# Block-sparse attention with a low-rank mixer: other queues for the first loads, first row copies cut by key chunk, pair 5 loaded earlier

## The chip, the cores and the metric

The kernel runs on one core of a Trainium2 chip. The metric is the device time of one execution in microseconds. Before the change, five runs gave a median of 284.89 us (283.51 to 286.13).

The engines are named as in the profile: PE is TensorE (matmuls; PEld is its weight load), DVE is VectorE, ACT is ScalarE, POOL is GpSimd and SP is SyncE. SP, ACT and POOL each have a queue from which DMAs are issued.

## The reference

Batch 4, 8 heads, 768 positions, head dimension 64. Attention is limited to blocks of 32: neighbours, the first and last row and column of blocks, and three sampled blocks in each row. Its output goes through a low-rank mix over positions and an MLP over 512 channels.

```python
mask = np.abs(blk_i - blk_j) <= 1
mask = mask | (blk_i == 0) | (blk_j == 0) | (blk_i == n_blocks - 1) | (blk_j == n_blocks - 1)
for qb in range(n_blocks):
    for kb in sampled_blocks[qb]:
        mask[qb * block:(qb + 1) * block, kb * block:(kb + 1) * block] = True
scores = np.where(mask, scale * np.matmul(q, k.transpose(0, 1, 3, 2)), -1e9)
attn = softmax(scores)                      # rows of 768
x = np.matmul(attn, v)                      # heads side by side: 4 x 768 x 512
u = x + (x.transpose(0, 2, 1) @ U @ V).transpose(0, 2, 1)       # rank 32
out = u + np.maximum(u @ w_ch1, 0.0) @ w_ch2                    # 512 -> 2048 -> 512
```

(`softmax` stands for the maximum, exponential, sum and division that the reference writes out.)

## The kernel before

**Tiling.** The heads are taken in pairs, 16 pairs in all, four for each batch entry. A sequence is laid out as 128 partitions by `T` = 6. For each head and each chunk `g` of 128 keys, PE multiplies the turned keys with the turned queries into PSUM (128 keys by 768 queries), ACT takes the exponential into a slot of `est`, and PE multiplies this by the values, with a column of ones that gives the sum (`value_product`, L400). DVE divides (`divide`, L472 and L477: one reciprocal and two products for each head).

**Two ways to mask.** For batch entry 0 (pairs 0 to 3) the mask is added by the matmul itself. The queries' tile `qres` has, beside the 64 data rows of a head, 24 rows with a one-hot code of the query's block, and the keys' tile `kres` has 24 rows with a bias of 0 or -240 for each key and query block. The bias is made at the start. `neq`, `a01` and `bias` (L289, L293, L296) come from the sampled blocks and from the constants in `small`. Two matmuls `mask_half` (L271) spread them over the 768 keys, and `mask_row` (L279) copies the result into the mask rows of `kres[0]`, for each head and each half of the keys. For pairs 4 to 15 the scores are unmasked, two chunks at once (`half_quad`, L741), and DVE multiplies the exponentials by a 0/1 mask (L756) that `mask_part` (L656, L662) makes during pairs 0 to 3.

**The start.** The first head of pair 0 is loaded by itself. `first_load` issues its DMA, `first_cast` converts it to 16 bits into `sts`, `first_turn` (L224) turns 3 chunks of 128 positions on PE, and `first_row` (L282) copies the turned rows into `qres[0]` or `kres[0]`. Eight matmuls on constants (`keep_warm`, L264) run on PE before that. The second head of pair 0 follows by `last_turn` (L337) and its copy (step `z`, L344). `second_set` copies the mask rows to `kres[1]` and `kmask` by DMA. The identity for turning, `id16`, lies in the same tile and the same DMA as the mask constants (`small`, 128 rows of 356 bytes).

**Order.** Inside `manual_schedule` each engine runs its instructions in the order in which the program issues them. After the start this order is the string `PLAN`, one word for each step, and a digit is the PSUM bank (of 8) that the step writes. Capitals are PE steps and small letters are the steps that empty them: `S` is a score block (2 banks) and `B` two blocks at once (3 banks), each with its exponential `e`; `A` is a value product of six matmuls, with `v` for the division; `R` is the turn of a later pair's queries or keys, with `t` for the row copies; `K`/`k` is a part of the 0/1 mask; `Z`/`z` is the turn of pair 0's second head; `M`/`m`, `X`, `Y`/`y`, `D`/`d` and `E`/`g` belong to the mix; `Q`, `H` are scores of pairs 4 to 15, with `e` and the mask product `p`; `V` is their value product; `U`, `P`, `C` are the first MLP matrix (L587) with relu `a` on ACT or `b` on DVE; `W`/`f` is the second (L611, L619).

**Loads.** `loads(i)` issues pair i+2's queries, keys and values on SP and casts them on POOL. From pair 5 on, `front(i+1)` ahead of it issues two DMA transposes of that pair's queries and keys. `begin(i)`, called when the first score of pair i is taken up, decides which loads are issued there. Pair 5's `loads(3)` is issued at the start of pair 3, and `front(5)` and `hold` (which lets POOL issue the `w2t` loads behind a copy that waits for pair 5's transposed keys) at the start of pair 4. The DMA transposes of the turned activations `uT` (L544) are on SP, too.

Of the kernel before, what the change touches and what calls it, by code (L numbers as in the profile page):

```python
# [12 lines left out]
FP32 = mybir.dt.float32  # L13
FP16 = mybir.dt.float16
# [5 lines left out]
P = 128  # L20
# [3 lines left out]
def kernel(  # L24
# [14 lines left out]
    nc = tc.nc  # L39
# [28 lines left out]
    small_np = np.zeros((P, NB + 1 + P // 2), np.float32)  # L68
    small_np[:NB, :NB] = (ms_np - 1.0) * -MASK_BIAS
    small_np[:NB, NB] = ii  # L70
    small_np[:, NB + 1 :] = np.eye(P, dtype=np.float16).view(np.float32)

    small_dr = nc.inline_tensor(small_np, name="small_const")
    ohT_dr = nc.inline_tensor(ohT_np, name="one_hot_const")
# [36 lines left out]
    small = consts.tile([P, NB + 1 + P // 2], FP32)  # L111
    ms = small[0:NB, 0:NB]
    iota = small[0:NB, NB : NB + 1]
    id16 = small[:, NB + 1 :].bitcast(FP16)
# [54 lines left out]
    def first_load(h, n, queue):  # L169

        src, nm = ((q, "qld"), (k, "kld"))[n]
        if h == 0:
            lds[nm] = ldpool.tile([P, 2, T, D], FP32, tag="ld" + nm, name=nm)
            sts[0, nm] = stpool.tile([P, T, 2, D], FP16, tag="st" + nm, name="st" + nm)
        if h == 1:
            nc.gpsimd.memset(lds[nm][0:1, h, 0, 0:1], 0.0)
        queue.dma_start(
            out=lds[nm][:, h], in_=src[0, h].rearrange("(p t) d -> p t d", t=T)
        )

# [4 lines left out]
    bias = consts.tile([P, 2, D], FP16)  # L185
    for vt in vts:
        nc.gpsimd.memset(vt[:, :, :, D : D + 1], 1.0)
# [3 lines left out]
    def second_set():  # L191
        for h in range(2):
            one_hot(1, h)
            nc.sync.dma_start(out=kres[1][mrows[h], h, :], in_=kres[0][mrows[h], h, :])
        nc.sync.dma_start(out=kmask[mrows[0], :], in_=kres[0][mrows[0], 0, :])
# [12 lines left out]
    def first_cast(h, n, copy):  # L208
        nm = ("qld", "kld")[n]
        copy(out=sts[0, nm][:, :, h], in_=lds[nm][:, h])  # L210
# [3 lines left out]
    def first_turn(n, c):  # L214

        if n == 1:
            pt = psm([P, HS], FP32)
        elif c == 0:
            pt = pw[:, 1, 0:HS]
        else:  # L220
            pt = psc2()[:, 0, 0:HS]
        first_out[n, c] = pt
        for j in range(3):
            nc.tensor.matmul(  # L224
                pt[0:D, j * P : (j + 1) * P],
                sts[0, ("qld", "kld")[n]][:, 3 * c + j, 0],
                id16,
                start=(j == 0), stop=(j == 2), skip_group_check=True,
            )

    with tc.manual_schedule(
# [13 lines left out]
        first_load(0, 0, nc.sync)  # L245
        nc.scalar.dma_start(out=small, in_=small_dr.ap())
        first_load(0, 1, nc.scalar)
        for h in (1, 0):
            nc.vector.memset(qres[0][(slice(D, P), slice(0, D))[h], h, :], 0.0)
            one_hot(0, h)  # L250
        nc.vector.memset(bias, 0.0)
# [26 lines left out]
        def mask_row(h, c, copy):  # L278
            copy(out=kres[0][mrows[h], h, c * HS : (c + 1) * HS], in_=pks[c][mrows[h]])  # L279

        def first_row(n, c, copy):
            copy(  # L282
                out=(qres, kres)[n][0][drows[0], 0, c * HS : (c + 1) * HS],
                in_=first_out[n, c][0:D],
            )

        neq = consts.tile([P, NB, 3], FP32)
# [14 lines left out]
        for n in range(2):  # L302
            first_cast(0, n, nc.vector.tensor_copy)
        for c in range(2):
            first_turn(0, c)
            first_row(0, c, nc.scalar.copy)
        mask_half(0)
        mask_row(0, 0, nc.vector.tensor_copy)
        first_turn(1, 0)
        first_row(1, 0, nc.scalar.copy)  # L310
        first_turn(1, 1)
        mask_half(1)
        keep_warm(2, 256)
        first_row(1, 1, nc.vector.tensor_copy)
        mask_row(0, 1, nc.vector.tensor_copy)
        mask_row(1, 0, nc.vector.tensor_copy)
        mask_row(1, 1, nc.vector.tensor_copy)
# [3 lines left out]
        nc.vector.memset(Ut, 0.0)  # L321
        load_v(0)
        load_qk(1)
        second_set()
        load_v(1)
        load_mix()


# [105 lines left out]
    S0 S3 e e S5 B0 e Z7 e S3 z Z6 e z B0 A7 A e R6 S3 t A R5 e A B0 t A K6 e A S3 k v A5 A e K6  # L434
    k B0 A A e K7 A K6 k S3 k A K7 e v B0 k S3 e M6 e A5 A m R7 A t B0 K6 R3 e k A A t S6 A e v
    S0 D2 S3 e d A7 A e A S0 K6 A e S3 k K2 A e S5 k A e v S3 R2 e S5 t S0 e M7 e S3 m D2 e B5 d
    A0 D1 e A A d A S3 D2 A e d K1 S5 k R7 e S3 t A S1 e v A5 A e A S3 S6 e K2 A e A k A S3 v B0
    e K7 M6 e k S3 m X5 K7 e A6 Y k A B0 y X7 Y e S3 y E5 A e A g A R7 S0 t A e v S4 S2 e A7 A e
    R1 E6 A t A g A A Q v e e M6 X7 m Y P6 y p H U7 e p H b C e p H b U7 e p H b U6 e p E1 a g p
    V7 Q v e e V6 U7 v p U0 a P1 b C p P6 a C E7 Q a g U6 e e U7 b P6 b p U0 C a U7 p a Q b X6 Y  # L440
    e e P7 y C P6 b C p U0 b a p V7 Q v e e V6 W7 v p U0 W a p Q U6 e e W b U6 p W b p Q f W6 e
    e W p U2 U0 a p a V7 Q v W e e p V7 U2 v W a p Q f W7 e e W p U6 W a p Q U6 e e W b U6 p f a
    p V0 U1 v a V7 U6 v Q a M6 e e W7 m W p D6 U0 d U1 p a D2 D3 a U6 d d D0 U5 a d D6 U1 a d W
    a W Q f D6 W7 e e d W p D0 D6 W d d p W Q f W6 e e W p W W p Q f e e V7 U6 v p a V0 U2 v p
    U7 a U6 a Q b U7 e e U6 b U7 b p U2 a U6 p a U7 a Q b U6 e e U7 b U6 b p U2 a p a V7 Q v e e
    V6 U7 v p U0 b U1 a W6 p a Q W e e W p W U7 f p Q a U6 e e W7 b W p U1 p a V6 Q v W e e p V6
    U2 v W a p Q f W6 e e W p U7 W b p Q U7 e e W b U7 p f U2 a p a V0 v V7 W6 v Q M7 e e W m U7
    p D0 U1 a d U2 p a D7 D3 a U0 d d U1 a D5 D0 a U2 d d U7 a W a W Q f D7 W6 e e d W p D1 D7 W
    d d p W Q f W7 e e W p W W p Q f e e V6 U7 v p a V0 U2 v p U7 a U6 a Q b U7 e e U6 b U7 b p
    U2 a U6 p a U7 a Q a U6 e e U7 b U6 b p U2 a p a V7 Q v e e V6 U7 v p U0 a U1 a U6 p a U7 a  # L450
    Q a W6 e e W p W U7 p Q a W e e W7 f p U0 b p V6 Q v W e e W p W U6 f p Q a U7 e e W6 b W p
    p V7 Q v W e e W p U7 f U0 a p a V1 v V3 U7 v U6 a M0 b U7 m U2 a D6 U0 a d D5 U1 a d D7 W4
    a d D6 D0 D1 d D2 d D3 d W d d U6 W a W W6 f W W W W7 f W W W U6 f U0 a U1 a U7 a U6 a U4 a
    U7 b U1 a U4 a W6 a W U7 U0 a U1 a U2 a U7 a U3 a U0 a U7 a U1 a U5 a U7 a W a U7 W a W4 f W
    U7 W b W U7 f U6 a U0 b U7 a W6 b U0 W b U7 U0 b W a U0 U7 b U1 b W a L4 f W2 l W W W W4 f W
    W W L7 f l
# [327 lines left out]
    def begin(i):  # L784
# [3 lines left out]
        if i == HP:  # L788
# [4 lines left out]
        for m in {0: (0,), 1: (1, 2), 3: (3,), 4: (4,)}.get(i, ()):  # L793
            loads(m)
        if i == HP:
            hold(kpl[1])
# [56 lines left out]
    with tc.manual_schedule(  # L853
# [7 lines left out]
        for word in PLAN.split():  # L861
# [39 lines left out]
```

## Time and profile before

| What | us |
|---|---|
| median of 5 runs | 284.89 (283.51 to 286.13) |
| profiled execution, time | 283.38 |
| its span | 281.5 |
| exponentials of two blocks (L724), x9, each | 1.45 to 1.47 |
| row copies of a later pair (L686), two for queries or keys | 1.11 to 1.14 |
| first MLP matrix (L587), x512, busy | 94.3 |
| second MLP matrix (L611), x368, busy | 87.1 |

The span runs from the first to the last instruction of the profiled execution, and its time has some 1.9 us more around it. Rows of the profile name the engine, the line, the operation, the tile written and the tiles read, and their shape; in square brackets stands how long the engine was idle before and which instruction released it. "ACTq" or "SPq" is the issue of a DMA from that queue. Matmuls overlap, so a row of six has a shorter time than the sum of its parts.

### The profile page before, as it was taken

What the parts mean: (1) busy time and instruction counts of PE and PEld (TensorE: products, weight loads), DVE (VectorE), ACT (ScalarE), POOL (GpSimd) and SP (SyncE); (2) the same over time, 40 slices, a digit from 0 to 9 for tenths busy, and PEclk for the clock granted to TensorE, in tenths of its full rate; (3) what the DMA queues carried; (4) which work ended last, traced back from release to release, by engine and by line L of the source; (5) the groups of instructions that cost most, each with busy time, mean ns of one, the idle gap of its engine ahead of it and who ended that gap; (6) DMA issues with size and microseconds to landing.
All of it is one profiled execution on the core that took longest, in us unless ns stands there. A gap on an engine that the chain in (4) does not pass through costs nothing.

```text
span 281.5 us, 6704 instructions
## 1 busy us (share of the span) xinstructions
PE 273.5 (97%) x2768; PEld 159.8 (57%) x2768; DVE 194.3 (69%) x347; ACT 177.9 (63%) x206; POOL 74.0 (26%) x164
## 2 busy tenths in 40 slices
PE   7899999999999999999999999999999999999993
PEld 3577775656465654656455654656547645555552
DVE  5699988988777898788677888776677871003411
ACT  3999998888668655686867555797776303451100
POOL 5378115905634050074352050060000000000000
PEclk9999999999999999999999999999999999999999
DMA  5799997999581653646351843740001062002021
GB/s 167 238 276 303 188 256 183 191 243 225 202 231 40 188 165 98 182 111 198 85 178 40 251 104 95 210 106 7 37 37 40 17 134 77 0 0 77 0 93 57
DMA packets 49119, 37.53 MB, mean 133 GB/s; under 512 B 30465, under 2 KB 45601, under 8 KB 49089
## 3 DMA queue, kind: packets, MB, share of 16 engines
q1 hardware_dynamic: 45968, 32.61, 41.5%
q0 software_dynamic: 2688, 4.19, 8.8%
q8 instruction: 21, 0.34, 0.5%
q10 hardware_dynamic: 432, 0.31, 0.3%
q14 instruction: 10, 0.07, 0.1%
HBM read 27.67 MB, written 6.29 MB: 121 GB/s over the span
## 4 chain that ended last, share of the span: by engine, by line
PE 92%; DVE 4%; DMA 2%; issue 1%; ACT 1%; SPq 0%; DVEq 0%; ACTq 0%
PE ps L587 30%; PE ps L611 29%; PE ps L400 12%; PE ps L741 10%; PE ps L697 3%; PE ps L716 2%; PE ps L529 2%; DMA qld<-in_q_dram 1%; PE ps L656 1%; DMA out_dram<-of 1%; DVE qres L686 1%; PE ps L636 1%; PE ps L670 1%; DVE kres L279 1%; ACT est L724 1%
## 5 line engine op out<-in xcount | busy, mean ns | idle before, releaser
L750 ACT ACTIVATE est<-ps 128x1536 f16<-128x1536 f32 x72 | 100.3, 1449 | 38.7 <-PE ps L741 38.7
L587 PE MATMUL ps<-uT,w1t 128*128 128x384 f16 x512 | 94.3, 326 | 0.0
L611 PE MATMUL ps<-w2t,tT 128*128 128x512 f16 x368 | 87.1, 379 | 0.0
L756 DVE TENSOR_TENSOR est<-est,mask 128x1536 f16<-128x1536 f16 x72 | 69.7, 972 | 15.0 <-ACT est L750 14.9
L599 ACT ACTIVATE tT<-ps 128x384 f16<-128x384 f32 x90 | 43.0, 494 | 43.5 <-PE ps L587 42.3
L587 PEld LDWEIGHTS <-w1t 128*128 128x128 f16 x512 | 47.6, 98 | 36.3 <-issue 5.8
L611 PEld LDWEIGHTS <-tT 128*128 128x128 f16 x368 | 34.5, 98 | 39.6 <-issue 3.8
L400 PEld LDWEIGHTS <-est 128*128 128x128 f16 x1152 | 40.8, 97 | 7.0 <-issue 1.9
L400 PE MATMUL ps<-vt,est 128*128 128x65 f16 x1152 | 43.4, 193 | 0.0
L140 POOL CAST stqld<-qld 128x192 f16<-128x192 f32 x40 | 15.4, 426 | 85.6 <-DMA qld<-in_q_dram 59.9
L619 DVE TENSOR_TENSOR of<-xf,ps 128x512 f32<-128x512 f32 x23 | 15.7, 684 | 27.7 <-PE ps L611 25.7
L601 DVE TENSOR_SCALAR tT<-ps 128x384 f16<-128x384 f32 x38 | 21.1, 556 | 18.6 <-PE ps L587 18.0
L741 PE MATMUL ps<-qpl,kpl 64*128 64x512 f16 (+1 forms) x288 | 31.3, 325 | 0.0
L706 ACT ACTIVATE est<-ps 128x768 f16<-128x768 f32 x30 | 22.5, 813 | 0.6 <-PE ps L697 0.6
L741 PEld LDWEIGHTS <-kpl 64*128 64x128 f16 x288 | 11.8, 94 | 15.9 <-issue 10.4
L140 POOL CAST stkld<-kld 128x192 f16<-128x192 f32 x40 | 19.4, 525 | 1.4 <-PE ps L587 1.2
L477 DVE TENSOR_TENSOR xh<-ps,rcp 128x384 f16<-128x384 f32 x32 | 17.8, 558 | 1.1
L477 DVE TENSOR_TENSOR xf<-ps,rcp 128x384 f32<-128x384 f32 x32 | 17.5, 548 | 0.0
L541 DVE TENSOR_TENSOR xh<-xh,ps 128x384 f16<-128x384 f16 x28 | 15.4, 550 | 1.7 <-PE ps L529 1.6
L542 DVE TENSOR_TENSOR xf<-xf,ps 128x384 f32<-128x384 f32 x28 | 15.4, 549 | 0.0
L140 POOL CAST vt<-vld 128x192 f16<-128x192 f32 x40 | 15.1, 417 | 0.4 <-DMA vld<-in_v_dram 0.4
L697 PE MATMUL ps<-qres,kres 128*128 128x384 f16 x60 | 14.0, 324 | 0.8 <-DVE kres L279 0.5
(83 smaller groups left out, 149.3 us busy)
## 6 DMA issues: line engine op xcount, KB each, us to landing
vld<-in_v_dram SPq DMA_DIRECT2D x16, 384.0 KB, 4.6
out_dram<-of SPq DMA_DIRECT2D x23, 256.0 KB, 2.1
qld<-in_q_dram SPq DMA_DIRECT2D x15, 384.0 KB, 5.1
kld<-in_k_dram SPq DMA_DIRECT2D x15, 384.0 KB, 4.9
w1t<-in_moe_w_ch_dram POOLq DMA_DIRECT2D x4, 512.0 KB, 9.0
w2t<-in_moe_w_ch_dram POOLq DMA_DIRECT2D x4, 512.0 KB, 7.7
qld<-in_q_dram SPq DMA_DIRECT2D x2, 192.0 KB
uT<-xh SPq DMA_TRANSPOSE x14, 2.8
```

Source lines behind the costliest of these rows:

```text
L140: last = nc.gpsimd.tensor_copy(out=dst[:, h, ts], in_=ld[:, h, ts])
L400: nc.tensor.matmul(pav[:, sc, :], est[:, n, sc * P : (sc + 1) * P], vts[b % 2][:, 2 * hp + h, g, 0 : D + 1], start=(g == 0 and sc == 0), s ...
L477: nc.vector.tensor_tensor(out=dst, in0=pav[:, :, 0:D], in1=rcp[:, :, None].broadcast_to([P, T, D]), op=ALU.mult,)
L587: nc.tensor.matmul(pt, w1t[:, cc, jj * P : (jj + 1) * P], bts[b].uT[cc][:, c * HS : (c + 1) * HS], start=(cc == 0), stop=(cc == NCC - 1), ...
L599: nc.scalar.activation(out=dst, in_=pt, func=AF.Relu)
L601: nc.vector.tensor_scalar_max(out=dst, in0=pt, scalar1=0.0)
L611: nc.tensor.matmul(po, tts[b, c, jj][:, s * P : (s + 1) * P], w2t[:, jj, :], start=(jj == 0), stop=(jj == NJJ - 1),)
L697: nc.tensor.matmul(ps[:, c], kT[:, h, g * P : (g + 1) * P], qT[:, h, c * HS : (c + 1) * HS], start=True, stop=True,)
L706: lambda: nc.scalar.activation(out=dst, in_=ps, func=AF.Exp, scale=0.125),
L741: nc.tensor.matmul(units[h][:, u * S + lo : u * S + hi], kT[drows[h], g * P : (g + 1) * P], qT[drows[h], lo:hi], start=True, stop=True, sk ...
L750: nc.scalar.activation(out=both[h], in_=units[h].rearrange("p (g n) -> p g n", g=2), func=AF.Exp, scale=0.125,)
L756: lambda: nc.vector.tensor_mul(out=both[h], in0=both[h], in1=mask[:, 2 * j : 2 * j + 2, :]),
```

## The change

1. The identity leaves `small` and becomes a constant and a tile of its own (`eye_const`, `id16`, 32 KB). `small` is now 24 rows of 25 numbers, and POOL issues its DMA, ahead of its memsets.
2. ACT's queue issues the first head's queries and then `id16`. SP's queue issues the sampled blocks, the first half of the first head's keys, the two one-hot codes and the second half of the keys.
3. `first_turn` uses PE's transpose into 16-bit PSUM in place of a matmul with the identity into 32-bit PSUM.
4. The first cast of the queries goes to ACT. The keys are cast in two halves on DVE. On PE the first `mask_half` stands ahead of the turns, and the two small `keep_warm` matmuls are gone.
5. `mask_row` and `first_row` can copy a part of the columns. The first 128 keys are copied ahead of the other 256 (on ACT and on DVE).
6. The second half of the keys (`second_keys`: its turn, its rows, the mask rows of head 1, the memset of `Ut`), `second_set`, `load_v(1)`, `load_mix` and `loads(0)` are issued behind the first two scores. Both one-hot codes of the second set go ahead of the other copies.
7. `loads(3)` (pair 5) is issued at the start of pair 2, so on SP ahead of the `uT` transposes. `front(5)` and `hold` are issued at the start of pair 3.
8. `PLAN` is written anew: the same steps in the same number (but 87 relus on ACT and 41 on DVE in place of 90 and 38), in another order and with other banks. Its beginning is shown below; each of its lines differs.

```diff
-    small = consts.tile([P, NB + 1 + P // 2], FP32)
+    small = consts.tile([P, NB + 1], FP32)
     ms = small[0:NB, 0:NB]
-    id16 = small[:, NB + 1 :].bitcast(FP16)
+    id16 = consts.tile([P, P], FP16)
...
-    def first_load(h, n, queue):
+    def first_load(h, n, queue, ts=slice(0, T)):
...
         queue.dma_start(
-            out=lds[nm][:, h], in_=src[0, h].rearrange("(p t) d -> p t d", t=T)
-        )
+            out=lds[nm][:, h, ts],
+            in_=src[0, h].rearrange("(p t) d -> p t d", t=T)[:, ts],
+        )
+    halves = (slice(0, T // 2), slice(T // 2, T))
...
+    nc.gpsimd.dma_start(out=small[0:NB], in_=small_dr.ap())
...
     def second_set():
         for h in range(2):
-            one_hot(1, h)
             nc.sync.dma_start(out=kres[1][mrows[h], h, :], in_=kres[0][mrows[h], h, :])
...
-            nc.tensor.matmul(
-                pt[0:D, j * P : (j + 1) * P],
-                sts[0, ("qld", "kld")[n]][:, 3 * c + j, 0],
-                id16,
-                start=(j == 0), stop=(j == 2), skip_group_check=True,
+            nc.tensor.transpose(
+                out=pt[0:D, j * P : (j + 1) * P],
+                in_=sts[0, ("qld", "kld")[n]][:, 3 * c + j, 0],
+                identity=id16,
             )
...
-        first_load(0, 0, nc.sync)
-        nc.scalar.dma_start(out=small, in_=small_dr.ap())
-        first_load(0, 1, nc.scalar)
+        first_load(0, 0, nc.scalar)
+        first_load(0, 1, nc.sync, halves[0])
+        nc.scalar.dma_start(out=id16, in_=eye_dr.ap())
         for h in (1, 0):
             nc.vector.memset(qres[0][(slice(D, P), slice(0, D))[h], h, :], 0.0)
             one_hot(0, h)
+        first_load(0, 1, nc.sync, halves[1])
...
+        first_cast(0, 0, nc.scalar.copy)
...
         keep_warm(8)
-        for n in range(2):
-            first_cast(0, n, nc.vector.tensor_copy)
+        first_cast(0, 1, nc.vector.tensor_copy, halves[0])
+        mask_half(0)
         for c in range(2):
             first_turn(0, c)
-            first_row(0, c, nc.scalar.copy)
-        mask_half(0)
-        mask_row(0, 0, nc.vector.tensor_copy)
         first_turn(1, 0)
-        first_row(1, 0, nc.scalar.copy)
-        first_turn(1, 1)
         mask_half(1)
-        keep_warm(2, 256)
-        first_row(1, 1, nc.vector.tensor_copy)
+        mask_row(0, 0, nc.vector.tensor_copy, 0, P)
+        first_row(0, 0, nc.scalar.copy)
+        first_row(0, 1, nc.vector.tensor_copy)
+        first_row(1, 0, nc.scalar.copy, 0, P)
+        first_row(1, 0, nc.vector.tensor_copy, P)
+        mask_row(0, 0, nc.vector.tensor_copy, P)
+        first_cast(0, 1, nc.vector.tensor_copy, halves[1])
         mask_row(0, 1, nc.vector.tensor_copy)
-        mask_row(1, 0, nc.vector.tensor_copy)
-        mask_row(1, 1, nc.vector.tensor_copy)
...
-        nc.vector.memset(Ut, 0.0)
         load_v(0)
         load_qk(1)
-        second_set()
-        load_v(1)
-        load_mix()
+        for h in range(2):
+            one_hot(1, h)
+    def second_keys():
+        first_turn(1, 1)
+        first_row(1, 1, nc.vector.tensor_copy)
+        for c in range(2):
+            mask_row(1, c, nc.vector.tensor_copy)
+        nc.vector.memset(Ut, 0.0)
...
-    S0 S3 e e S5 B0 e Z7 e S3 z Z6 e z B0 A7 A e R6 S3 t A R5 e A B0 t A K6 e A S3 k v A5 A e K6
+    S0 S3 e e Z7 S0 z Z2 e B3 z S6 e B0 e e A5 A A A A A R6 v S3 t e B0 R7 e S4 t K3 A6 e A k B0
...
-        if i == HP:
+        if i == HP - 1:
             front(HP + 1)
...
-        for m in {0: (0,), 1: (1, 2), 3: (3,), 4: (4,)}.get(i, ()):
+        for m in {1: (1, 2), 2: (3,), 4: (4,)}.get(i, ()):
             loads(m)
-        if i == HP:
+        if i == HP - 1:
             hold(kpl[1])
...
-        for word in PLAN.split():
+        for x, word in enumerate(PLAN.split()):
+            if x == 2:
+                second_keys()
+                second_set()
+                load_v(1)
+                load_mix()
+                loads(0)
```

## The prediction

> **What bounds the kernel now.** I read the engines' totals and slices first, then the busy time by stage, then the first microseconds instruction by instruction.
>
> ```profile
> PE 273.5 (97%) x2768; PEld 159.8 (57%) x2768; DVE 194.3 (69%) x347; ACT 177.9 (63%) x206; POOL 74.0 (26%) x164
> ACT  3999998888668655686867555797776303451100
> ```
>
> Over the whole run TensorE is the bound, but the slices show ScalarE full from the second to the sixth. The stages, one row each (span of us, length, busy us and instructions of PE, PEld, DVE, ACT, POOL, then granted clock, DMA share, GB/s):
>
> ```profile
> 7.40:16.60 9.20, 7.89 (x106) 5.60 (x105) 6.63 (x14) 8.54 (x9) 4.83 (x6) 1.00 0.76 238
> 16.60:43.20 26.60, 26.25 (x393) 19.78 (x390) 24.08 (x55) 25.62 (x30) 11.39 (x16) 1.00 1.02 251
> 76.00:220.00 144.00, 144.00 (x1550) 81.87 (x1552) 111.00 (x183) 100.82 (x109) 35.73 (x90) 1.00 0.42 119
> 220.00:277.00 57.00, 57.00 (x372) 31.95 (x367) 19.04 (x36) 14.21 (x29) 0.00 (x0) 1.00 0.17 50
> ```
>
> From 7.4 to 43.2 us (the 48 score blocks of pairs 0 to 3) ScalarE's exponentials pace the work: it is idle for 0.66 us up to 16.6 and 0.98 us of the next 26.6. From 76 us on TensorE never pauses. So what the change does to the start counts only as far as it moves ScalarE's whole row of exponentials, and the diff leaves TensorE's later work the same in amount. The start:
>
> ```profile
> 0.79 3.47 PE L264 MATMUL ps<-const-bfloat16-1.0 128*128 128x512 bf16 x8 [0.79 <-PEq L885]
> 1.25 0.38 SPq L177 DMA_DIRECT2D qld<-in_q_dram  x1
> 3.35 0.36 SPq L177 DMA_DIRECT2D qld<-in_q_dram  x1
> 4.75 0.36 DVE L210 CAST stqld<-qld 128x384 f16<-128x384 f32 x1 [1.23 <-DMA qld<-in_q_dram]
> 5.17 0.52 PE L224 MATMUL ps<-small,stqld 128*64 128x128 f16 x6 [0.92 <-DVE stqld L210]
> 5.56 0.85 ACT L282 CAST qres<-ps 64x384 f16<-64x384 f32 x2 [2.40 <-PE ps L224]
> 6.84 0.99 PE L697 MATMUL ps<-qres,kres 128*128 128x384 f16 x5
> 7.38 2.21 ACT L706 ACTIVATE est<-ps 128x768 f16<-128x768 f32 x3 [0.59 <-PE ps L697]
> 10.42 0.56 DVE L344 COPY kres<-ps 64x768 f16<-64x768 f16 x1 [0.17 <-PE ps L337]
> 16.62 1.45 ACT L724 ACTIVATE est<-ps 128x1536 f16<-128x1536 f32 x1 [0.20 <-PE ps L716]
> ```
>
> The queries, second in SP's queue, land just before 4.75, are turned from 5.17, and the first score runs at 6.84, its exponential at 7.38. Pair 1's first exponential starts at 16.62. That is the mark by which I judge the start.
>
> **The change, step by step (us from the span's start).**
>
> *Operands.* The queries are issued on ScalarE at 0.74 instead of 1.25. From issue to landing the trace has 2.0 (the small constants, 44.5 KB) and 3.8 (the keys, 192 KB); I take 3.0, as half of the key traffic has been put off: 3.7. ScalarE has its table load and dummy behind it at 3.15. It casts the queries in 0.48 (its row of 384 columns): done at 4.2. The first half of the keys, issued on SP at 1.18, lands at 4.2 by the same 3.0, and VectorE's half cast (half of 0.36) ends at 4.4. At 3.8 instead of 3.0 the queries would be 0.7 late. At 2.0 nothing is gained, because the 8 warm-up matmuls hold TensorE until 4.26.
>
> *Mask constants on GpSimd's queue.* Now issued at 0.75. mask_half(0) is the first instruction behind the warm-up, so everything queues behind it on TensorE. Bounds from issue to landing: 2.0 (the same constants from ScalarE's queue) and 6.4 (the fastest of four 512 KB weight loads from GpSimd's queue). 25 columns of 24 rows are nearest the first; I take 2.7: 3.45, plus 0.64 for the three VectorE steps (2.89 to 3.53 in the trace) gives 4.1, in time. Landing at 6.4 would give 7.8 and put everything 3.5 later. The issue also takes GpSimd about 0.67 (its first weight-load issue), so its marker memsets of the second heads' buffers end that much later. SP's load of the second queries, which waits for one, goes out near 4.0 instead of 3.35, and the second keys, v and pair 1 behind it slip by as much. Their casts stay ahead of use: second queries land 2.2 to 3.0 later, 6.2 to 7.0, plus a cast of 0.5, against use at 7.44 below.
>
> *The skill on this queue.* The row first: four software-queue loads took 6.4 to 12.4 us for 512 KB, and no small one exists. The Trainium skill, "DMA: Bandwidth & Descriptors", section "Anatomy of one DMA — SWDGE (gpsimd) path", fits about 2.0 us plus bytes over 436 GB/s; by it the constants land at 2.8 and the sum is unchanged. Against the change stands "SBUF — State Buffer", section "SBUF: two separate sides": while VectorE runs an operation in a two-port mode, GpSimd cannot write such descriptors. If VectorE's memsets (0.89 to 2.96) counted as such, landing would be some 2.96 + 2.0 = 5.0, bias 5.6, and the start 1.4 later, an estimate from that page that would eat the lead. No row of before shows which holds.
>
> *First score.* From 4.26: mask_half 0.2, six query turns 0.36, three key turns 0.2, the second mask_half 0.2. ScalarE copies the first query half 0.39 behind its first turn (5.17 to 5.56): 4.85, for 0.43, then 128 key columns, between 0.20 (its one-column dummy) and 0.48, say 0.28: done 5.56. VectorE copies 128 mask columns (0.28, its 128-column cast at L502), then the second query half from 5.03. The new PSUM type is 16-bit: 768 such columns took 0.56, and 384 of 32-bit 0.55, so 384 of 16-bit lie between 0.28 and 0.55; I take 0.36: 5.39. First score 5.60, exponential 5.60 + 0.54 = 6.14. Lead over 7.38: 1.24. The two removed keep-warm matmuls lay in a wait and give nothing.
>
> *Where the lead goes.* VectorE's queue from there: rest of key rows 5.56 to 5.88, rest of mask rows 6.30, half cast 6.5, mask_row(0,1) 7.05, first_row(1,1) 7.40, the two mask rows of head 1 8.5, Ut 8.87, and the two z copies 9.43 and 9.99 (0.55 to 0.56 each, as L279 and L344). Z7 stands before the third score on TensorE and uses the bank that first_row(1,1) empties: 7.44, third score 7.8, exponential 8.34, though ScalarE is free at 7.62 (2 x 0.74): 0.72 idle. Z2 needs the bank that mask_row(1,1) empties: 8.54, the double score 8.9, its exponential 0.86 later (11.04 to 11.90 in the trace) at 9.76, with ScalarE free at 9.06: 0.70 idle. Then 1.45 and 0.74, so head 1's first exponential starts at 11.95; in before at 11.90. The lead is spent.
>
> *Up to pair 1.* Value products wait for the double exponential (11.21). The new order runs all six before pair 1's query turn, and VectorE does the division (0.2 + 0.56 + 0.55 = 1.16 as seen) from 12.45, then four row copies at 0.56: 15.85. Pair 1's first exponential 0.86 later, 16.7, against 16.62: +0.1. VectorE has then done a division more and a mask copy and a half less, so it stands 0.3 ahead.
>
> *Pair 5.* Its three 384 KB loads go from SP at 35.8 to behind pair 4's, before the two uT transposes (29.75 on, held 3.9 by their data). 1.15 MB at 251 GB/s is 4.6 us of DMA time put where the share is already 1.02 and w1 is loading. The cover is large: first use of w1 is at 45.3, of w2 at 68.2; pair 5's own rows are first read near 52.8. Without that cover the 4.6 would show. The uT transposes wait for VectorE anyway. GpSimd's casts of pair 5 go from 41 to near 28, where it is less than half busy (11.39 of 26.60), and the w2 loads behind its hold copies start earlier too: 0.
>
> *Rest.* Pair 4's key turn and copy (42.0 to 43.2 in before) are no longer next to the first Q, which still waits for the last value product: 0 to -0.35, I take -0.1. Three relus move from ScalarE (0.49) to VectorE (0.56), neither full there: 0. Sum: +0.1 - 0.1 = 0.0.
>
> **Own time and median.** The profiled execution took 283.38 (span 281.5 plus 1.9 around it), below the median of 284.89. With a sum of 0.0, and small slack on VectorE, 284.8 in medians.
>
> **The rivals.**
> A, likeliest: no change, 284.8. For it: VectorE's chain at 7 to 10 us and at 13 to 16. Its own range 283.7 to 286.0, by the 16-bit copies (three on the chain, -0.2 to +0.5), the landing (up to +0.7) and ScalarE's gaps (0.98 less at most).
> B, faster: ScalarE keeps the lead. If second-half copies are near 0.28 and the gaps at 7.6 and 9.1 close, -1.24, the seam -0.1, and a third of the later 0.98 idle: 284.89 - 1.7 = 283.2. For it: ScalarE has no slack in before, and any lead kept there is carried on. Against: VectorE's sum of ten operations, counted above.
> C, slower: the rewritten order starves ScalarE between 16.6 and 43.2. A reused bank that VectorE has not emptied costs 0.7, as at 7.6 and 9.1; the new order reuses banks 1 and 2 after divisions in pair 2. Three such holes: +2.1, 287.0; it decides from two. For it: VectorE busy 24.08 of 26.60. Against: I followed pairs 1 and 2 and found pair 2's first double score near 29.9 in both.
> D: the mask constants land late. Each microsecond beyond 3.6 delays the first score, and all that VectorE does behind it, by one, and the lead is spent already: from 5.0 the loss passes 1.4, and at 7.15 (0.75 + 6.4) it is 3.5, 288.3. For it: the constants stand first on TensorE now. Against: the transfer is tiny.
>
> **How the numbers follow.** A 0.48, B 0.24, C 0.20, D 0.08. About 0.5% (1.4 us) is what a measurement can tell. Faster beyond it: B but for 0.02, 0.22. Slower: C and D, 0.28. Same: 0.50. Range: A whole, down to B's 283.2 less a little, up to C's 287.0: 282.9 to 287.0.
>
> **What would show it.** First exponential near 6.1, ScalarE idle some 0.7 before its third and fourth, head 1's first at about 12, pair 1's first near 16.7, first Q near 43. If pair 1's first is at 15.5, B; if ScalarE idles over 2.5 in 16.6 to 43, C; if mask_half(0) starts after 5, D. I am wrong in all if the time moves beyond 76 us, where TensorE was full.

## The result, and the profile after

The changed kernel takes 286.49 us in the median of 37 runs (284.35 to 290.35), the kernel before 284.90 in 72 runs beside it (283.25 to 288.64). The ratio is 1.0047, 95% interval 1.003 to 1.0064: slower by about 1.3 us (the medians differ by 1.6). The profiled execution took 285.46 us, with a span of 283.5, against 283.38 and 281.5 before. Both lie below their medians, that of before among its fastest 22 times, so the two profiles differ by 2.1 us, a little more than the medians.

The page's totals and ScalarE's row of slices, then busy time by stage, with the columns and stages of before:

```profile
PE 275.7 (97%) x2766; PEld 159.9 (56%) x2766; DVE 196.6 (69%) x353; ACT 177.4 (63%) x203; POOL 76.5 (27%) x165
ACT  3699997897776656687667546598876300443200
```

```profile
7.40:16.60 9.20, 8.15 (x88) 4.74 (x87) 5.95 (x15) 7.13 (x8) 3.98 (x7) 1.00 0.75 222
16.60:43.20 26.60, 25.87 (x372) 19.22 (x371) 24.26 (x53) 25.33 (x29) 13.56 (x18) 1.00 1.05 263
76.00:220.00 144.00, 143.90 (x1515) 80.88 (x1513) 111.89 (x183) 100.45 (x106) 39.85 (x96) 1.00 0.44 120
220.00:277.00 57.00, 57.00 (x382) 31.74 (x381) 21.73 (x42) 14.25 (x29) 0.00 (x0) 1.00 0.18 54
```

From 76 us on TensorE is as full as before. The loss is in the first stage: ScalarE (the fourth pair of numbers) works 7.13 us of 9.20 where it worked 8.54, 1.41 less. The timeline of the changed kernel's start:

```profile
0.79 3.57 PE L265 MATMUL ps<-const-bfloat16-1.0 128*128 128x512 bf16 x8 [0.79 <-PEq L899]
1.25 0.70 POOL L189 DMA_DIRECT2D small<-small_const  x1 [0.79 <-POOLq L899]
4.44 0.22 DVE L294 TENSOR_TENSOR neq<-sb,small 24x72 f32<-24x72 int32 x1 [1.48 <-DMA small<-small_const]
5.20 0.50 PE L272 MATMUL ps<-qres,bias 24*128 24x384 f16 x1 [0.84 <-DVE bias L301]
5.62 0.85 PE L225 MATMUL ps<-id,stqld 128*64 128x128 f16 x6
7.16 1.58 PE L705 MATMUL ps<-qres,kres 128*128 128x384 f16 x4
8.01 1.57 ACT L714 ACTIVATE est<-ps 128x768 f16<-128x768 f32 x2 [0.92 <-PE ps L705]
10.49 0.81 ACT L714 ACTIVATE est<-ps 128x768 f16<-128x768 f32 x1 [0.91 <-PE ps L705]
11.74 1.45 ACT L732 ACTIVATE est<-ps 128x1536 f16<-128x1536 f32 x1 [0.44 <-PE ps L724]
18.48 1.45 ACT L732 ACTIVATE est<-ps 128x1536 f16<-128x1536 f32 x1 [0.20 <-PE ps L724]
```

GpSimd issues the mask constants at 1.25, and `neq`, which needs them, starts at 4.44 after a wait of 1.48 (2.89 in before). The bias follows, and `mask_half(0)` begins at 5.20, with TensorE idle for 0.84 behind the eight warm-up matmuls. The first exponential starts at 8.01 (7.38 in before), pair 1's first at 18.48 (16.62).

The same marks carry the whole span:

| us | before | after | loss so far |
|---|---|---|---|
| first exponential | 7.38 | 8.01 | 0.63 |
| pair 1's first exponential | 16.62 | 18.48 | 1.86 |
| first exponential of pair 4 (`Q`) | 44.31 | 46.64 | 2.33 |
| end of the span | 281.5 | 283.5 | 2.0 |

Nearly all of it is there by pair 1. The next question is what TensorE ran at. In the row of 5.62, six turns take 0.85 us, 0.107 from one to the next; before, the same six took 0.52 (0.055 apart). So TensorE worked at half speed here, and at the first scores: four in 1.58 us, where five took 0.99. Behind them the last three turns at half speed and the first six at full speed are these:

```profile
8.67 0.53 PE L225 MATMUL ps<-id,stkld 128*64 128x128 f16 x3
9.64 0.49 PE L345 MATMUL ps<-id,stqld 128*128 128x128 f16 x6 [0.44 <-DVE kres L286]
```

Half speed is also what TensorE has at the start of these runs: the eight warm-up matmuls start 0.427 us apart from the second on, for 512 columns, in both kernels, as long for each column (0.83 ns) as 0.107 us for 128. Before, TensorE was at full speed when the turns came at 5.17. In the changed kernel it got there only at about 9 us. The profile's granted clock does not show this: it reads 1.00 for the whole start, but its records begin only at 9.12 us here (4.01 in before), and time ahead of the first record counts as 1.00. So for this execution the half speed is read from the spacing of the matmuls.

The answer for the tile `small` says who was held up by its DMA (us, times):

```profile
who waited for it (us, times):
  PEld L272: 1.7, 1
  DVE neq L294: 1.5, 1
  PE ps L272: 0.8, 1
...
DMA to landing us min/median/max: 3.2/3.2/3.2
```

### The profile page after: what moved, and what is told of

It is laid out like the page before. It is cut to its first block, busy times and chain, and to the rows that moved or that the text cites. A ratio compares the mean times of both kernels' runs of the same rounds, so it can differ in the third digit from the quotient of the medians.

```text
span 283.5 us, 6707 instructions
## 1 busy us (share of the span) xinstructions
PE 275.7 (97%) x2766; PEld 159.9 (56%) x2766; DVE 196.6 (69%) x353; ACT 177.4 (63%) x203; POOL 76.5 (27%) x165
## 4 chain that ended last, share of the span: by engine, by line
PE 89%; ACT 3%; DVE 3%; DMA 2%; issue 1%; DVEq 0%; ACTq 0%; POOLq 0%
PE ps L595 30%; PE ps L619 29%; PE ps L408 11%; PE ps L749 10%; PE ps L705 2%; ACT est L732 2%; PE ps L537 2%; PE ps L724 2%; ACT est L714 1%; DMA small<-small_const 1%; DMA out_dram<-of 1%; PE ps L644 1%; PE ps L664 1%; PE ps L225 1%; PE ps L506 1%
## 5 line engine op out<-in xcount | busy, mean ns | idle before, releaser
L607 ACT ACTIVATE tT<-ps 128x384 f16<-128x384 f32 x87 | 41.8, 494 | 45.2 <-PE ps L595 34.4
L140 POOL CAST stqld<-qld 128x192 f16<-128x192 f32 x40 | 20.0, 548 | 87.3 <-DMA qld<-in_q_dram 39.0
L609 DVE TENSOR_SCALAR tT<-ps 128x384 f16<-128x384 f32 x41 | 22.8, 556 | 28.5 <-PE ps L595 27.6
L140 POOL CAST stkld<-kld 128x192 f16<-128x192 f32 x40 | 16.9, 476 | 0.7 <-POOL stqld L140 0.7
L140 POOL CAST vt<-vld 128x192 f16<-128x192 f32 x40 | 16.1, 468 | 0.0
L705 PE MATMUL ps<-qres,kres 128*128 128x384 f16 x60 | 14.6, 337 | 0.5 <-ACT est L714 0.2
```

The lines of the kernel that those rows point to most:

```text
L140: last = nc.gpsimd.tensor_copy(out=dst[:, h, ts], in_=ld[:, h, ts])
L607: nc.scalar.activation(out=dst, in_=pt, func=AF.Relu)
L609: nc.vector.tensor_scalar_max(out=dst, in0=pt, scalar1=0.0)
L705: nc.tensor.matmul(ps[:, c], kT[:, h, g * P : (g + 1) * P], qT[:, h, c * HS : (c + 1) * HS], start=True, stop=True,)
```

## The experiments

Each kernel was timed 12 times beside runs of the kernel before on the same chip; the median of before in those runs stands in brackets.

### Constants back on ScalarE's queue, and alone on GpSimd's

Run `a_consts_act` is the changed kernel with the constants issued by ScalarE, between the queries and the identity:

```diff
-    nc.gpsimd.dma_start(out=small[0:NB], in_=small_dr.ap())
...
         first_load(0, 0, nc.scalar)
         first_load(0, 1, nc.sync, halves[0])
+        nc.scalar.dma_start(out=small[0:NB], in_=small_dr.ap())
         nc.scalar.dma_start(out=id16, in_=eye_dr.ap())
```

> The changed kernel with the mask constants issued from ScalarE's queue, right behind the queries, in place of GpSimd's. Theory 1 (the constants land at 4.4 us instead of 3.45, hold mask_half(0), the first instruction on TensorE behind the warm-up, until 5.2, and everything behind it): VectorE's first step on them starts near 3.0 to 3.5, first exponential at 6.0 to 6.6 (8.01 in the changed kernel), pair 1's first at 16.5 to 17.0 (18.48), time 1.5 to 2.0 us below the changed kernel, ratio to before 0.996 to 1.001. Theory 2 (the rewritten order and the moved loads cost the time): pair 1's first exponential may move, but the time stays at a ratio near 1.004 to 1.006.

Measured: 283.95 us (284.49), ratio 0.9983 (0.9955 to 1.001). One DMA moved, and the loss is gone. Its timeline (the marks come a tenth of a microsecond or so behind those expected):

```profile
3.66 0.22 DVE L294 TENSOR_TENSOR neq<-sb,small 24x72 f32<-24x72 int32 x1 [0.70 <-DMA small<-small_const]
4.46 0.47 PE L272 MATMUL ps<-qres,bias 24*128 24x384 f16 x1
6.69 1.58 ACT L714 ACTIVATE est<-ps 128x768 f16<-128x768 f32 x2 [0.59 <-PE ps L705]
9.13 0.81 ACT L714 ACTIVATE est<-ps 128x768 f16<-128x768 f32 x1 [0.86 <-PE ps L705]
17.12 1.45 ACT L732 ACTIVATE est<-ps 128x1536 f16<-128x1536 f32 x1 [0.20 <-PE ps L724]
```

`neq` starts 0.78 earlier, TensorE shows no idle time in brackets ahead of `mask_half(0)`, and pair 1 starts at 17.12.

Run `b_consts_pool` does the opposite: the kernel before, with only this part of the change (and the identity in a tile of its own).

```diff
+    nc.gpsimd.dma_start(out=small[0:NB], in_=small_dr.ap())
...
-        nc.scalar.dma_start(out=small, in_=small_dr.ap())
+        nc.scalar.dma_start(out=id16, in_=eye_dr.ap())
```

> The kernel before with one part of the change alone: identity in a tile of its own from ScalarE's queue, mask constants from GpSimd's queue. Here mask_half(0) stands behind the query turns at 5.69 us. Theory 1 (the constants count by their landing alone): the bias is ready near 5.15, the first mask_half is not late, ratio 0.999 to 1.001. Theory 1b (GpSimd's queue counts too: its marker memsets end 1.2 us later and with them SP's loads of the second head, v and pair 1): the turn of the second head's queries, at 9.16 in before, goes to about 9.9, and the time rises by 0.5 to 1.2 us, ratio 1.002 to 1.004.

Measured: 285.43 us (284.49), ratio 1.0056 (1.0026 to 1.0086): this one part makes the kernel before as slow as the whole change does, and costs more than either theory had (up to 1.004). Its stages (span, length, busy us of the five engines, granted clock, DMA share, GB/s) show the second thing that the late constants do:

```profile
3.40:6.80 3.40, 1.75 (x17) 0.89 (x15) 1.54 (x6) 0.80 (x3) 1.17 (x5) 1.00 0.49 161
6.80:10.20 3.40, 3.40 (x13) 1.60 (x13) 2.68 (x6) 2.15 (x5) 1.83 (x3) 0.51 0.92 308
10.30:13.60 3.30, 2.58 (x34) 1.82 (x33) 1.12 (x2) 2.87 (x4) 0.83 (x1) 1.00 0.57 167
```

VectorE's casts stand behind `neq` there, so TensorE waits 1.65 us for the cast queries. It is busy for only 1.75 of the 3.4 us, and in the next 3.4 us the granted clock is 0.51. Then it is full again. Here full speed was reached and lost; in the profile of the changed kernel it was reached late.

### The pause behind the warm-up, filled

If the half clock is a part of the price, filling TensorE's pause should give that part back while the constants stay late. Run `c_warm` adds one line to the changed kernel, run `i_before_warm` adds it to the kernel before:

```diff
         keep_warm(8)
+        keep_warm(4, 256)
```

> The changed kernel with four more warm-up matmuls of 256 columns behind the eight, so that TensorE's pause of 0.84 us before the late mask_half(0) is filled. The constants stay late. Theory 1 (late constants alone): mask_half(0) stays at 5.2 us, the turns behind it keep their 0.107 us spacing or not without effect on the time, ratio as the changed kernel, 1.003 to 1.006. Theory 4 (the pause also costs the clock: with it TensorE runs the turns and first scores at half speed, spacing 0.107 instead of 0.055 us): turns at 0.055, first exponential 0.4 to 0.8 us earlier than 8.01, time 0.4 to 1.0 us below the changed kernel, ratio 1.000 to 1.003.

> The kernel before with the same four warm-up matmuls. Theory 4: the pause of 0.91 us there (4.26 to 5.17) costs the clock in some executions, which is why its times lie in groups near 283.4, 284.8 and 286.0; filled, the group near 283.4 holds most, median below 284.0, ratio 0.996 to 0.999. If the clock does not matter: ratio 0.999 to 1.001.

Measured: `c_warm` 284.81 us (284.00), ratio 1.0028 (0.9999 to 1.0056); `i_before_warm` 283.52 (284.00), ratio 0.9963 (0.9934 to 0.9992). The second is a gain in a kernel that computes and orders everything as before. All its 12 times lie between 282.97 and 283.92. The 72 of the kernel before, which has a pause of 0.92 us at the same place, come in steps: 22 at 283.25 to 283.68, 23 at 284.39 to 285.07, the other 27 from 285.73 up. The changed kernel has 6 of 37 in its lowest step (284.35 to 284.71), and its fullest step is at 286.4 to 286.9. In the timeline of `c_warm`:

```profile
4.17 0.22 DVE L294 TENSOR_TENSOR neq<-sb,small 24x72 f32<-24x72 int32 x1 [1.20 <-DMA small<-small_const]
4.92 0.33 PE L272 MATMUL ps<-qres,bias 24*128 24x384 f16 x1 [0.18 <-DVE bias L301]
5.19 0.52 PE L225 MATMUL ps<-id,stqld 128*64 128x128 f16 x6
6.80 1.58 ACT L715 ACTIVATE est<-ps 128x768 f16<-128x768 f32 x2 [0.59 <-PE ps L706]
```

The constants are late, though by 0.27 less than in the changed kernel's profile, the six turns take 0.52, and from `mask_half(0)` to the first exponential it is 1.88 us instead of 2.81. So the profile of the changed kernel pays twice: for the late constants themselves, and for a clock that a pause at this place leaves at half speed in some executions.

The clock alone does not set the two kernels apart, though. With the pause filled in both, on the same chip, every time of `i_before_warm` (283.92 at most) lies below every time of `c_warm` (284.15 at least), and the medians are 1.29 us apart. The kernel before pays for its own pause as well. What filling gives back to the changed kernel is not clear of noise in `c_warm` (its interval overlaps 1.003 to 1.0064). It is clearer with pair 5's old due times (below): `n_oldloads`, with the pause, has five of its twelve times at 286.3 to 287.9 and one at 289.0, and `o_warm_oldloads`, with the pause filled, on the same chip, has none above 285.02. The profile of `n` (286.54) is one of the five. Its pair 1 starts at 18.16, that of `o` at 17.23, and ahead of that its granted clock is near half:

```profile
7.00:10.40 3.40, 2.92 (x19) 1.94 (x20) 3.02 (x7) 1.73 (x3) 1.84 (x3) 0.53 0.98 300
```

### The start, the order and GpSimd's other work

Four runs split the change in other ways. `d_start_only` has the changed start with the old `PLAN` and due times, `e_plan_only` the old start with the new ones:

```diff
-    S0 S3 e e Z7 S0 z Z2 e B3 z S6 e B0 e e A5 A A A A A R6 v S3 t e B0 R7 e S4 t K3 A6 e A k B0
+    S0 S3 e e S5 B0 e Z7 e S3 z Z6 e z B0 A7 A e R6 S3 t A R5 e A B0 t A K6 e A S3 k v A5 A e K6
...
```

> The changed kernel's start (queues, halves, 16-bit turns, split copies, second keys behind two scores) with the plan of before and its due times of the pair 5 loads, transposes and w2 hold. Theory 1 (the start, by its late constants, costs it all): ratio 1.003 to 1.007, first exponential near 8.0. Theory 2 (order and loads cost it): ratio 0.996 to 1.001.

> The start of before with the changed kernel's plan and its due times of the loads. Theory 1: the first exponential stays at 7.38 and the time within 0.5 us of before plus what the order adds behind pair 1 (0.47 us between 18.48 and 46.64 in the changed kernel), ratio 1.000 to 1.002. Theory 2: ratio 1.004 to 1.007.

Measured: 285.59 (284.49), ratio 1.0041 (1.001 to 1.0071), and 284.23 (284.49), ratio 1.0033 (0.9997 to 1.0069). The start alone is slower; for the order alone the ratio and the medians disagree (284.23 is below 284.49), and it is left unclear.

GpSimd's issue also delays its markers, and with them SP's loads of the second head (4.55 us instead of 3.35). `j_markers_late` (the kernel before) and `l_act_markers_late` (run `a`) have that delay without the late constants, by three more memsets ahead of the markers:

```diff
+    for _ in range(3):
+        nc.gpsimd.memset(kmask.bitcast(FP32), 0.0)
```

> The kernel before with three more memsets of kmask on GpSimd ahead of its others, so that the marker memsets of the second heads' buffers end 1.2 us later, as in the changed kernel, while the constants stay on ScalarE's queue. Theory 1 (VectorE and TensorE wait for the constants themselves): ratio 0.999 to 1.002. Theory 1b (SP's loads behind the markers are what is late): second head's turn at 10 us or later instead of 9.16, ratio 1.002 to 1.004, half or more of what the constants on GpSimd cost the kernel before (1.0056).

> a_consts_act (constants on ScalarE's queue, no pause behind the warm-up) with the three memsets that put the marker memsets, and SP's loads of the second head, v and pair 1, 1.2 us later. This separates the two things that the constants on GpSimd's queue do, without the pause that moves the clock. Theory 1 (the constants' landing): time as a_consts_act, 283.7 to 284.2 us. Theory 1b (the later loads): 284.5 to 285.2, as c_warm (284.81), with the second head's turn and the third exponential later than 9.13 by 0.5 us or more.

Measured: `j` 285.44 (284.00), ratio 1.0032 (0.9995 to 1.0069), inconclusive, with a lowest time (283.48) near that of before, and with TensorE at half speed up to about 10 us in its profile (286.67); `l` 284.01 (284.50), ratio 0.9964 (0.9936 to 0.9991). In `l` the marker memset runs at 4.30 and SP's load goes out at 4.42, yet the median is that of `a` (283.95). The later markers and loads cost nothing there. In `b`, how much of 0.0056 they cost stays open, since 0.0032 of `j` is more than half of it and its interval reaches below 1.

`k_scores_first` is `a` with the first four scores ahead of the second head's turns; `m_scores_first_warm` adds two narrow keep-warm matmuls behind the second `mask_half`; `f_consts_act_oldplan` is `a` with the old order and due times:

```diff
-    S0 S3 e e Z7 S0 z Z2 e B3 z S6 e B0 e e A5 A A A A A R6 v S3 t e B0 R7 e S4 t K3 A6 e A k B0
+    S0 S3 e e S0 e B3 e Z7 z Z2 z S6 e B0 e A5 A A A A A R6 v S3 t e B0 R7 e S4 t K3 A6 e A k B0
...
         mask_half(1)
+        keep_warm(2, 256)
```

> The changed kernel with the constants on ScalarE's queue and the beginning of its plan turned round: the third score and the double score stand ahead of the second head's turns (S0 S3 e e S0 e B3 e Z7 z Z2 z S6 e B0 e A5 in place of S0 S3 e e Z7 S0 z Z2 e B3 z S6 e B0 e e A5). If the lead of the start was lost where the turns wait for banks (ScalarE idle 0.86 and 0.44 us before its third and fourth exponentials): these gaps shrink to under 0.4 in sum, head 1's first exponential at 11.2 to 11.7 instead of 12.42, pair 1's first at 16.0 to 16.6 instead of 17.12, ratio 0.994 to 0.998. If VectorE's chain sets pair 1's start anyway: pair 1 stays near 17.1 and the ratio at 0.998.

> k_scores_first with two warm-up matmuls of 256 columns behind the second mask_half, as the kernel before had them ahead of its first scores. If TensorE's pauses there (5.6 to 6.1 us) cost the clock in some executions: the few runs of k_scores_first above 284 us go, median 282.8 to 283.1, ratio 0.993 to 0.997. If not: as k_scores_first, 0.997.

> a_consts_act with the plan and the due times of before: the new start without its late constants, under the old order. If the new order is what spends the lead: pair 1's first exponential at 15.8 to 16.3 us and 283.0 to 283.4. If the old order spends it as well (its first double score and second-head turns stand in the same banks): pair 1 at 16.8 or later, 283.8 to 284.5.

Measured: `k` 283.09 (284.00), ratio 0.9974 (0.9941 to 1.0007); `m` 283.28 (284.50), ratio 0.9949 (0.9919 to 0.9978); `f` 283.10 (284.50), ratio 0.9949 (0.992 to 0.9978). `m` and `f` beat both kernels. Since filling the pause alone gave the kernel before 0.9963, part of this can be the clock. The two keep-warm matmuls of `m`, which stood at this place before the change, did not do what was expected of them: four of its times lie above 284, where three of `k`'s do, and the ratios of the two overlap. In `f` the first exponential starts at 6.33, 1.05 ahead of before, and pair 1's first at 16.62, as in before to the hundredth: the lead is spent under the old order too (neither expectation had this mark together with this time). In `k` the third exponential follows without the wait:

```profile
6.61 2.30 ACT L714 ACTIVATE est<-ps 128x768 f16<-128x768 f32 x3 [0.59 <-PE ps L705]
9.09 1.45 ACT L732 ACTIVATE est<-ps 128x1536 f16<-128x1536 f32 x1 [0.18 <-DVE kres L280]
16.40 1.45 ACT L732 ACTIVATE est<-ps 128x1536 f16<-128x1536 f32 x1 [0.34 <-PE ps L724]
```

Three exponentials run back to back (2.30 us), the fourth waits 0.18 instead of 0.44, and pair 1 starts at 16.40 against 17.12 in `a`.

### Pair 5's loads

Due times put back as before, in `a` (`h_consts_act_oldloads`), in the changed kernel (`n_oldloads`), in `c_warm` (`o_warm_oldloads`, with `c2_warm`, which is `c_warm` again, beside it on the same chip) and in `m` (`p_scores_warm_oldloads`):

```diff
-        if i == HP - 1:
+        if i == HP:
...
-        for m in {1: (1, 2), 2: (3,), 4: (4,)}.get(i, ()):
+        for m in {1: (1, 2), 3: (3,), 4: (4,)}.get(i, ()):
```

> a_consts_act with the due times of before for pair 5's loads, its transposes and the w2 hold. My prediction put the earlier loads at nothing: 283.7 to 284.3 us, within 0.3 of a_consts_act. If they matter: more than 0.5 us from it, either way.

> The changed kernel with four narrow keep-warm matmuls behind the eight, a second time, as the partner of the next run. Theory U (pair 5's loads, issued ahead of the transposes of uT, hold up the second of these): its issue on SP again takes 6 to 9 us instead of 2 to 4, it lands between 44 and 47.6 us, and where it lands after 46.5 TensorE waits for it; some 284.8 against 284.5 of the kernel before. Rival (the loads cost nothing, the 0.81 us wait of the first look was a single event): the same median, with no wait for uT in the profile.

> The same with the due times of pair 5's loads, transposes and hold as before the change. Theory U: the second transpose of uT takes 2 to 4 us to issue, no wait of TensorE for uT, and the median is 0.4 to 0.9 below that of its partner. Rival: the medians of the two agree within 0.2.

> The changed kernel with the due times of pair 5's loads, transposes and hold as before the change, and the constants still late. Theory: the start is as late as in the changed kernel (neq near 4.4, pair 1's first exponential at 17.2 to 18.5 by the clock), so most of the loss stays: 285.4 to 286.2 where the kernel before has 284.5. Rival (the loads are the loss, the constants are not): 284.5 or less.

> Constants on ScalarE's queue, the first four scores ahead of the second head's turns, two keep-warm matmuls behind the second mask_half, and pair 5's loads as before the change. Theory U: second transpose of uT at 2 to 4 us, the median 0.3 to 0.8 below the same kernel with early loads (283.3): 282.5 to 283.0, ratio 0.991 to 0.994. Rival: 0.995, as with the early loads.

| early loads | median, ratio | old due times | median, ratio |
|---|---|---|---|
| `a` | 283.95, 0.9983 | `h` | 283.44, 0.9974 (0.9942 to 1.0006) |
| `c2` | 285.04, 1.001 (0.9977 to 1.0043) | `o` | 284.55, 0.9976 (0.9946 to 1.0006) |
| changed kernel | 286.49, 1.0047 | `n` | 285.48, 1.0018 (0.9976 to 1.006) |
| `m` | 283.28, 0.9949 | `p` | 282.89, 0.9929 (0.9895 to 0.9962) |

The old due times are lower in all four pairs, by 0.4 to 1.0 us in the medians and by 0.0009 to 0.0034 in the ratios. No single pair settles it by its ratios, whose intervals overlap; but in the only pair that ran on one chip, six of `c2`'s twelve times lie above the highest of `o`'s (285.02). The queue of SP shows where the early loads weigh. The second transpose of `uT` from the changed kernel, then from `h`, then TensorE in `c_warm`:

```profile
34.13 5.69 SPq L552 DMA_TRANSPOSE uT<-xh  x1
```

```profile
32.44 2.26 SPq L552 DMA_TRANSPOSE uT<-xh  x1
```

```profile
47.66 0.32 PE L596 MATMUL ps<-uT,w1t 128*128 128x384 f16 x1 [0.81 <-DMA uT<-xh]
```

The issue of the second transpose takes 4.8 to 9.0 us in the eight profiles with early loads, and 1.4 to 4.0 in the ten without. In `c_warm` (9.03, ending at 41.9) it landed too late, and TensorE stood for 0.81 us. In `a` it landed 12.0 us after its issue at 32.8, so at 44.8, 1.3 before the row at 46.1 whose second matmul reads it. `c2` did not repeat the wait (5.60), so the expectation of it failed there; but VectorE was caught in another one, shown with GpSimd's casts beside it:

```profile
49.72 3.58 DVE L765 TENSOR_TENSOR est<-est,mask 128x1536 f16<-128x1536 f16 x1
...
49.52 1.25 POOL L140 CAST stqld<-qld 128x192 f16<-128x192 f32 x4
50.68 1.23 POOL L140 CAST stkld<-kld 128x192 f16<-128x192 f32 x4
51.82 1.96 POOL L140 CAST vt<-vld 128x192 f16<-128x192 f32 x4
```

One mask product took 3.58 us where the median of 72 is 0.96, while GpSimd ran twelve casts without a break. That the casts held it is not shown: in the changed kernel the same twelve casts run without a break beside products of 0.95 to 0.96, and there eight of the casts are slow (2.80 and 2.73 us for four). In `o` GpSimd's `w2t` issues stand between the casts and the products stay below 1.2. The old due times have a risk of their own: in `n` TensorE waited 1.27 us for `w2t` at 76.31, and in `j` 1.52, and `n` has its times from 286.3 up. But `o` has the same due times and neither the wait nor such times, so the due times alone do not make them. So the early loads are the dearer choice by about half a microsecond, but by stalls in some executions; the profiles of the changed kernel, of `a` and of `l` show none of them. That typical executions lose by this is not shown.

## Why the prediction was wrong

**The term that failed: the landing of the mask constants.** The prediction took 0.75 for the issue and 2.7 to the landing, 3.45. Measured are 1.25 and 3.2, 4.44. This is its rival D with its sign (`mask_half(0)` at 5.20, after 5), which had a chance of 0.08 since "the transfer is tiny". The other runs that issue the constants from GpSimd have `neq` at 4.11 to 4.58, so this was no single event. The price bounds of 2.0 to 6.4 held 3.2; what was not counted is that GpSimd starts to issue half a microsecond after the other queues (its issue row waits 0.79 for its sequencer). Of the two estimates that were set beside each other there, neither fits. The Trainium skill, "DMA: Bandwidth & Descriptors", section "Anatomy of one DMA — SWDGE (gpsimd) path", fits 2.0 us plus the bytes: from 1.25 that is 3.25, 1.2 too early. "SBUF — State Buffer", section "SBUF: two separate sides", has descriptors locked out while VectorE holds the shared port: the estimate of 5.0, which took VectorE's memsets for such a case, was 0.6 too late, though nearer. No run here moved VectorE's memsets to tell which of the two is at work.

**The term that was missing: TensorE's clock.** From 4.26 on the sum takes every step of TensorE at the speed it had in the profile of before (six turns 0.36), and has no term for a start at half speed. From `mask_half(0)` to the first exponential it has 1.88 us; `c_warm` measured 1.88, and the changed kernel 2.81. The sum for the profiled execution closes: first exponential 8.01 instead of 6.14, of which 0.94 is `mask_half(0)` at 5.20 instead of 4.26, and 0.93 the half speed. How the loss in the medians divides between the two is open, since the kernel before has such a pause too. The profiles with TensorE at full speed from the turns on give an estimate for the late constants alone: `c_warm` and `c2_warm` have their first exponential at 6.80 and 6.96 where `h`, with the constants in time, has it at 6.36, and pair 1's first at 17.23 and 17.39 where `h` has 16.79, so 0.44 to 0.60 us.

That the two removed keep-warm matmuls "lay in a wait and give nothing" is not refuted. They stood further on, at 6.61 in before, not in the pause behind the eight; no run puts them alone back into the changed kernel, and in `m` two such matmuls gave nothing clear of noise.

**What held.**
- From the first exponential to pair 1's first one the prediction counts 10.56 us (6.14 to 16.7). It is 10.47 in the changed kernel and 10.43 in `a`. The two gaps of 0.72 and 0.70 are 0.86 and 0.44 in `a`. The division that is written as 0.2 + 0.56 + 0.55 = 1.16 adds up to 1.31; 1.16 is right, since the rows overlap (1.17 in the changed kernel, 14.62 to 15.79).
- "The lead is spent": `f` (old order) and `h` (new order) start 1.05 and 1.02 ahead of before (6.33, 6.36) and reach pair 1 at 16.62 and 16.79 against 16.62.
- With the constants in time, the forecast of no change is what `a` measures (0.9983, interval across 1). Some of that may be luck: `a` also lost the pause, which by itself gave the kernel before 0.9963, and pays for pair 5's early loads; the prediction counted neither.
- That 286.49 lies below the 287.0 of the range is luck. The 287.0 was rival C's price for three holes that are not there.
- GpSimd's markers slip 1.2 us instead of the 0.67 counted, and SP's loads go out at 4.55; that this is hidden holds (`l`).

**What was a little off.** VectorE's cast of half the keys took 0.33 us, not half of 0.36. From pair 1's to pair 4's first exponential: 27.69 us before, 28.16 after, +0.47 where -0.1 was taken for the seam; 27.83 in `a`. From there to the end the changed kernel is 0.33 shorter (236.86 against 237.19), which nothing here explains. Rival C's starving is therefore at most this 0.47, and none of its three holes of 0.7 is there. Rival B needed gaps that close; `k` closes them by another order.

**Pair 5, taken at 0.** "The uT transposes wait for VectorE anyway" explains the time up to the second one's issue (34.13 in the changed kernel), but not the issue itself and the landing, which were longer wherever pair 5's 1.15 MB of loads went ahead of them in the queue. The cover is down to 1.3 us in `a` and gone in `c_warm`. The cover that the prediction named was that of w1, w2 and pair 5's own rows; the tile late next was `uT`. It is the likely second part of the loss (0.4 to 1.0 us by the four pairs), the constants, with what they do to the clock, being the first: `a` alone takes 0.0064 off the ratio, `n` alone 0.0029.

The fastest kernel found is `p`: constants on ScalarE's queue, four scores first, two keep-warm matmuls behind the second `mask_half`, and pair 5 as before, at 282.89 us, ratio 0.9929.

## What to carry to other kernels

When a step is moved to the head of an engine's order, its operand becomes the one that must land first: read when that queue really starts to issue, not only how long the transfer is. A matmul that only fills a pause right behind the warm-up is not idle ballast: see how far apart equal matmuls start on each side of the pause, and if times come in steps, try a few more of them. For a DMA that goes ahead of others in a queue, list the landing of everything that it overtakes, small transposes included, against their first use.

## What the runs showed of the hardware

- **The clock changes in whole stretches.** In `b_consts_pool` the granted clock is 1.00 for 3.4 us, 0.51 for 3.4 us and 1.00 again, behind a stretch in which TensorE was busy for half the time. This agrees with the Trainium skill, "TensorE: Matmul & The Clock Gate", section "🔬 Part 1: The HAM clock gate (the "warmup" mystery)", which has a free-running window of about 3.4 us, so that the same kernel meets it at another phase in each run. The profiles agree: the changed kernel reaches full speed at about 9 us, `j` at about 10 and `before` by 5.17, with pauses of 0.84, 0.89 and 0.92. That could give the steps of 1.1 to 1.4 us in the times of before; filling the pause removed them (`i_before_warm`), but no run ties each step to a phase.
- **A first DMA from GpSimd's queue is late twice.** Issue at 1.25 us, where ScalarE's queue issued at 0.75; 3.2 us to the landing of 24 rows of 100 bytes (`neq` at 4.11 to 4.58 over seven runs). From ScalarE's queue, issued at 1.2 as well, `a` had them in use at 3.66 (3.48 to 3.66 over seven runs).
- **One product of VectorE took 3.58 us beside GpSimd's casts.** The same product takes 0.96 in the median of `c2_warm`, and in the other profiles 1.22 at most. The Trainium skill, "SBUF — State Buffer", section "SBUF: two separate sides", describes an exclusive lock on the port that the two share, held for a whole instruction; the one event agrees with it, but no run here provoked it on purpose.
